# Moving the wait for the output DMAs behind the exit barrier in a two-part decode-attention kernel

## The chip, the cores and the metric

The kernel runs on one core of one Trainium2 chip. The metric is the device time of an execution in microseconds (us). A kernel is run several times. The profile shows one execution. Its *span* is the time from its first to its last instruction record, and it is shorter than the device time: what the runtime does before the first and after the last instruction has no records.

The engines are PE (TensorE), DVE (VectorE), ACT (ScalarE), POOL (GpSimd) and SP (SyncE, which issues nearly all DMAs here). A trailing q, as in POOLq, is an engine's sequencer.

## The reference

Two decode steps of attention for one token, one with a sliding window (A) and one over the whole cache (B), put side by side:

```python
# B = 1, Sq = 1, D = 576, 32 query heads, 16 key/value heads, cache of 8192 x 128, bfloat16
q = (x @ wq) as 32 heads of 128
scores = q . k * 128**-0.5          # A: the last 2048 positions, B: all 8192
o = softmax(scores) @ v
a_or_b = o as [1, 1, 4096] @ wo     # -> 576 values
return concatenate([a, b], axis=-1) # -> [1, 1, 1152]
```

## The kernel before

A small helper class records every operation with what it reads and writes, derives the semaphore waits, and then emits each engine's list inside one block. Only the end matters here.

```python
class Program:
    def emit(self):
        ...
        def plain(eng, ops):
            for op in ops:
                for key in sorted(op.left, key=str):
                    eng.wait_ge(self.sem(key), op.left[key][1])
                one(eng, op)
        ...
        with self.nc.Block() as block:      # its exit is a barrier of all five engines
            @block.sync
            def _(sp):
                run("sp", sp)
            @block.gpsimd
            def _(pool):
                run("pool", pool)
            ...                             # tensor, vector, scalar

...
    def finish_out(P):
        add("dve", lambda dve: dve.tensor_copy(outsb[:, P, :], ktps[P][:, 0:OUTW]), ...)
        ...
        add("sp", put, reads=[("outsb", P)], writes=[("out", P)], dma="out%d" % P)   # 1.1 KB to memory
...
    for P in range(2):
        for Q, lo, n, view, res, after in wo_loads:
            if Q == P:
                wo_part(P, lo, n, view, res)     # matmuls with the output weights, as they land
        finish_out(P)
    add("sp", lambda sp: sp.nop(), reads=[("out", 0), ("out", 1)])   # wait for both output DMAs
    prog.emit()
```

In the profile the block's exit has line L248: each engine drains, reports to GpSimd with a semaphore, and GpSimd releases all (its two EVENT_SEMAPHORE records).

Of the kernel before, what the change touches and what calls it, by code (L numbers as in the profile page):

```python
# [38 lines left out]
class Program:  # L39
# [15 lines left out]
    def add(self, eng, fn, reads=(), writes=(), dma=None, after=(), tag=None, inc=1, loop=None):  # L55
        op = Op(eng, fn, tuple(reads), tuple(writes), dma, tag, 16 if dma is not None else inc, loop)
        deps = []
        for r in op.reads:
            w = self.writer.get(r)
            if w is not None:  # L60
                deps.append((w, True))
            if r[0] == "bank":
                deps += [(o, False) for o in self.readers.get(r, ())]
        for r in after:
            deps += [(o, False) for o in self.readers.get(r, ())]
        for r in op.writes:
            w = self.writer.get(r)
            if w is not None:
                deps.append((w, False))
            deps += [(o, False) for o in self.readers.get(r, ())]  # L70
        for r in op.reads:
            self.readers.setdefault(r, []).append(op)
        for r in op.writes:
            self.writer[r] = op
            self.readers[r] = []
        for o, raw in deps:
            if o is op:
                continue
            if o.dma is None and o.eng == eng and (not raw or eng in ("pe", "sp")):
                continue  # L80
            op.deps.append(o)
            o.needed = True
        op.order = len(self.ops)
        self.ops.append(op)
        return op
# [184 lines left out]
def bass_concat_heads__sliding_block_cached__gqa_block_cached__decode_kernel(  # L270
# [27 lines left out]
    prog = Program(nc)  # L298
    add = prog.add
# [351 lines left out]
    def finish_out(P):  # L651
        add("dve", lambda dve: dve.tensor_copy(outsb[:, P, :], ktps[P][:, 0:OUTW]), reads=[("bank", P)],  # L652
            writes=[("outsb", P)])

        def put(eng):
            src = bass.AP(tensor=outsb, offset=P * OUTW, ap=[[32 * 2 * OUTW, 4], [1, OUTW]])
            dst = out[0, 0:1, P * DM:(P + 1) * DM].rearrange("o (j n) -> (o j) n", j=4)
            return eng.dma_start(dst, src)
        add("sp", put, reads=[("outsb", P)], writes=[("out", P)], dma="out%d" % P)


    for P in range(2):
# [11 lines left out]
        reads=["mask0", ("rows", 0)], writes=["maskS", "rows"])  # L674
# [47 lines left out]
    for P in range(2):  # L722
# [1 line left out]
            if Q == P:  # L724
                wo_part(P, lo, n, view, res)
        finish_out(P)
    add("sp", lambda sp: sp.nop(), reads=[("out", 0), ("out", 1)])
    prog.emit()

# [1 line left out]
_INS = ['A_x', 'A_k_cache', 'A_v_cache', 'A_wq', 'A_wo', 'B_x', 'B_k_cache', 'B_v_cache', 'B_wq', 'B_wo']  # L731
# [24 lines left out]
```

## Time and profile before

| | before |
|---|---|
| device time, median | 250.03 us (249.70 to 250.25, 5 runs) |
| span of the profiled execution | 247.66 us |
| memory traffic | 102.9 MB, 416 GB/s |
| end of the last matmul to the last record | 2.46 us (245.21 to 247.66) |

From the page of the kernel before, the span, the busy times and three rows of the table of 40 slices (tenths of busy time; GB/s moved):

```profile
span 247.7 us, 7505 instructions
...
PE 169.6 (68%) x3406; PEld 132.3 (53%) x3406; DVE 81.0 (33%) x152; ACT 87.1 (35%) x92; POOL 12.9 (5%) x49
...
PE   0193589994999559995999638998345144685634
...
DMA  7999999999999999999999999999999999999993
GB/s 270 406 433 431 430 431 421 426 423 429 431 425 429 426 421 431 422 431 434 423 429 429 423 431 429 426 437 426 429 429 423 431 426 429 434 427 427 421 406 138
```

The DMA engines are full in all slices but the first and last. The kernel is bound by memory traffic up to its last weights; only the first and the last few microseconds are anything else.

The end of it, from the timeline (start in us, duration in us, engine, line, operation):

```profile
245.26 0.31 DVE L652 CAST outsb<-ktps 128x144 bf16<-128x144 f32 x1 [10.17 <-PE ktps L646]
245.59 0.56 SPq L658 DMA_DIRECT2D out_dram<-outsb  x1
```

The wait for the outputs (L727) and the barrier at the block's exit (L248) by source line: engine, operation, count, shortest/median/longest duration in ns, and the starts of the first and the last in us:

```profile
L727 SPq EVENT_SEMAPHORE  x1: 17/17/17, 247.2 to 247.2; - x1
```

```profile
L248 POOLq EVENT_SEMAPHORE  x2: 17/17/17, 247.5 to 247.6; - x2
L248 POOLq DRAIN  x1: 322/322/322, 137.8 to 137.8; - x1
L248 ACTq DRAIN  x1: 326/326/326, 212.6 to 212.6; - x1
L248 PEldq DRAIN  x1: 370/370/370, 244.9 to 244.9; - x1
L248 DVEq DRAIN  x1: 347/347/347, 245.3 to 245.3; - x1
L248 SPq COMPARE_BRANCH  x1: 33/33/33, 247.3 to 247.3; - x1
L248 SPq DRAIN  x1: 13/13/13, 247.4 to 247.4; - x1
L248 SPq EVENT_SEMAPHORE  x1: 17/17/17, 247.6 to 247.6; - x1
L248 ACTq EVENT_SEMAPHORE  x1: 17/17/17, 247.6 to 247.6; - x1
L248 DVEq EVENT_SEMAPHORE  x1: 21/21/21, 247.6 to 247.6; - x1
L248 PEldq EVENT_SEMAPHORE  x1: 51/51/51, 247.6 to 247.6; - x1
```

And SyncE's waits (in us, count, longest):

```profile
SPq L727 <- DMA out_dram<-outsb: 1.0, 1, 1.0
...
SPq L248 <- PEq L248: 0.2, 1, 0.2
```

The order can be read off the starts. SyncE issues the last output DMA at 245.59 us. Its wait is met at 247.2 (247.217 in the instruction record, 1.63 us after the issue began). Only then does SyncE drain and report to the barrier, and GpSimd releases everyone at 247.6.

"Behind the issue" below means behind the start of the last output DMA. Figures with three decimals are from the instruction records of the traces, which the views round.

### The profile page before, as it was taken

The page shows a single profiled execution, that of the slowest core. Times are in us where ns is not written, and L with a number is a line of the kernel's source. Part 1 is how long each engine was busy: PE and PEld are TensorE (multiplying, and loading weights), DVE is VectorE, ACT ScalarE, POOL GpSimd, SP SyncE. Part 2 cuts the span into 40 slices and gives each one's busy share as a digit, 9 for nine tenths or more (in the row PEclk, how much of TensorE's full clock was granted, in tenths as well). Part 3 has the DMA queues.
Part 4 walks back from the last instruction along what each step waited for, and adds up shares of the span by engine and source line. Part 5 has one row for each costly group of instructions (what it writes and reads, how often), then busy time and mean ns, then how long its engine had stood idle before and what let it go on. Part 6 is the DMA issues. An engine that isn't in the chain of part 4 may idle for free. (4 is left out here: it accounts for less than half of the span.)

```text
span 247.7 us, 7505 instructions
## 1 busy us (share of the span) xinstructions
PE 169.6 (68%) x3406; PEld 132.3 (53%) x3406; DVE 81.0 (33%) x152; ACT 87.1 (35%) x92; POOL 12.9 (5%) x49
## 2 busy tenths in 40 slices
PE   0193589994999559995999638998345144685634
PEld 0031288763877458864878428785244142584522
DVE  0001225554555017564555122655004004204000
ACT  2000047767478009786578004775200000000000
POOL 7501000000000000000000000000000000000000
PEclk9999959999799979998899955999858755557555
DMA  7999999999999999999999999999999999999993
GB/s 270 406 433 431 430 431 421 426 423 429 431 425 429 426 421 431 422 431 434 423 429 429 423 431 429 426 437 426 429 429 423 431 426 429 434 427 427 421 406 138
DMA packets 8235, 102.92 MB, mean 416 GB/s; under 512 B 1184, under 2 KB 1312, under 8 KB 2080
## 3 DMA queue, kind: packets, MB, share of 16 engines
q1 hardware_dynamic: 7936, 102.77, 98.0%
q8 instruction: 8, 0.13, 0.2%
q10 hardware_dynamic: 288, 0.00, 0.1%
q14 instruction: 3, 0.02, 0.0%
HBM read 102.76 MB, written 0.00 MB: 415 GB/s over the span
## 5 line engine op out<-in xcount | busy, mean ns | idle before, releaser
L472 ACT ACTIVATE kt<-ktps 128x1024 bf16<-128x1024 bf16 x80 | 77.9, 1021 | 54.5 <-PE ktps L466 54.4
L466 PEld LDWEIGHTS ktps<-ident,kslots 128*128 128x128 bf16 x1280 | 78.9, 103 | 27.9 <-issue 27.9
L466 PE MATMUL ktps<-ident,kslots 128*128 128x128 bf16 x1280 | 85.1, 230 | 12.4 <-PEq L214 12.4
L475 DVE COPY kt<-ktps 128x1024 bf16<-128x1024 bf16 x80 | 55.2, 691 | 53.7 <-PE ktps L466 53.6
L557 PE MATMUL opsum<-vslots,ptm 128*32 128x128 bf16 x1280 | 28.1, 262 | 28.0 <-PEq L214 23.7
L557 PEld LDWEIGHTS opsum<-vslots,ptm 128*32 128x32 bf16 x1280 | 25.3, 119 | 31.6 <-issue 31.6
L486 PE MATMUL sacc<-kt,qst 128*32 128x512 bf16 x320 | 25.3, 392 | 1.8 <-PEq L214 1.8
L566 DVE TENSOR_TENSOR diag<-opsum,rows 128x512 f32<-128x512 f32 x5 | 3.5, 691 | 55.9 <-PE opsum L557 55.9
L425 PE MATMUL opsum<-vslots,xpad 128*32 128x512 bf16 x64 | 8.2, 489 | 14.8 <-DVE xpad L410 12.1
L599 ACT ACTIVATE stat<-stat 128x1 f32<-128x1 f32 (+1 forms) x2 | 0.6, 294 | 37.2 <-DVE stat L597 37.2
L425 PEld LDWEIGHTS opsum<-vslots,xpad 128*32 128x32 bf16 x64 | 2.3, 119 | 17.6 <-issue 13.1
L457 POOL COPY qst<-qtm 128x64 bf16<-128x64 bf16 x20 | 4.5, 236 | 123.2 <-PE sacc L486 113.5
L646 PE MATMUL ktps<-kslots,opj 128*32 128x144 bf16 x184 | 6.1, 326 | 5.8 <-DMA kslots<-in_B_wo_dram 3.9
L486 PEld LDWEIGHTS sacc<-kt,qst 128*32 128x32 bf16 x320 | 5.1, 94 | 8.2 <-issue 4.4
L431 ACT ACTIVATE qrow<-opsum 128x512 bf16<-128x512 f32 x2 | 1.2, 597 | 23.1 <-PE misc L425 23.1
L523 ACT ACTIVATE psb<-sacc,stat 128x2048 bf16<-128x2048 f32 x3 | 5.9, 1967 | 8.5 <-DVE stat L517 8.5
L646 PEld LDWEIGHTS ktps<-kslots,opj 128*32 128x32 bf16 x184 | 5.2, 145 | 6.4 <-DMA kslots<-in_B_wo_dram 4.2
L425 PE MATMUL misc<-vslots,xpad 128*32 128x512 bf16 x64 | 8.2, 487 | 0.0
L630 PE MATMUL misc<-acc,pick 128*128 128x32 f32 x16 | 3.8, 404 | 3.6 <-DVE acc L624 2.9
L433 DVE CAST qrow<-misc 128x512 bf16<-128x512 f32 x2 | 1.4, 692 | 14.6 <-PE misc L425 14.6
L652 DVE CAST outsb<-ktps 128x144 bf16<-128x144 f32 x2 | 0.6, 307 | 16.0 <-PE ktps L646 16.0
L630 PEld LDWEIGHTS misc<-acc,pick 128*128 128x128 f32 x16 | 3.6, 328 | 3.8 <-DVE acc L624 3.0
(66 smaller groups left out, 62.1 us busy)
## 6 DMA issues: line engine op xcount, KB each, us to landing
kslots<-in_B_k_cache_dram SPq DMA_DIRECT2D x16, 2048.0 KB, 19.6
vslots<-in_B_v_cache_dram SPq DMA_DIRECT2D x16, 2048.0 KB, 18.4
kslots<-in_A_k_cache_dram SPq DMA_DIRECT2D x4, 2048.0 KB, 29.8
vslots<-in_A_v_cache_dram SPq DMA_DIRECT2D x4, 2048.0 KB, 23.5
vslots<-in_A_wq_dram SPq DMA_DIRECT2D x2, 2048.0 KB, 9.9
vslots<-in_B_wq_dram SPq DMA_DIRECT2D x2, 2048.0 KB, 19.6
kslots<-in_A_wo_dram SPq DMA_DIRECT2D x2, 2016.0 KB, 23.8
kslots<-in_B_wo_dram SPq DMA_DIRECT2D x1, 2016.0 KB, 31.2
```

The lines of the kernel that those rows point to most:

```text
L425: ins = pe.matmul(qps[c][32 * j:32 * j + 32, :], lhsT=xpad[:, P, x, :], rhs=src[:, o:o + 512], start=(u == 0), stop=(u == WQ_UNITS - 1))
L433: add("dve", lambda dve: dve.tensor_copy(qrow[:, 512:1024], misc[:, :]), reads=[B_M], writes=[("qrow", 1)])
L457: add("pool", lambda pool: pool.tensor_copy(qst[:, s * 64:(s + 1) * 64], qtm[:, o:o + 64]), reads=[("qtm", KIND[g])], writes=[("qst", s)], ...
L466: ins = pe.matmul(ktps_bf[q][:, t * 128:(t + 1) * 128], lhsT=kslots[:, s, o:o + 128], rhs=ident[:, :], start=True, stop=True, is_transpose ...
L472: add("act", lambda act, q=q, dst=dst: act.activation(dst, ktps_bf[q], ACT.Copy), reads=[("bank", q)], writes=[("kt", u % NKT, q)], tag="e ...
L475: add("dve", lambda dve, q=q, dst=dst: dve.tensor_copy(dst, ktps_bf[q]), reads=[("bank", q)], writes=[("kt", u % NKT, q)], tag="e%d%d" % ( ...
L486: ins = pe.matmul(sacc[32 * j:32 * j + 32, 512 * half:512 * half + 512], lhsT=qst[:, s * 64 + e * 32:s * 64 + e * 32 + 32], rhs=rhs, start ...
L523: return act.activation(psb[:, :].rearrange("p (x g) -> p x g", g=2), src, ACT.Exp, bias=st(P, C_NB + k), scale=SCALE, accum_out=st(P, C_L ...
L557: ins = pe.matmul(opsum[32 * j:32 * j + 32, s * DH:(s + 1) * DH], lhsT=ptm[:, o:o + 32], rhs=vslots[:, s, b * 128:(b + 1) * 128], start=(u ...
L566: return dve.tensor_tensor(diag[:, g % 2, :, :], opsum[:, :].rearrange("p (s d) -> p d s", s=NS), m, ALU.mult)
L630: ins = pe.matmul(misc[:, 0:32], lhsT=pick[:, r, :], rhs=acc[:, d, 32 * r:32 * r + 32], start=(r == 0), stop=(r == 3))
L646: ins = pe.matmul(ktps[P][32 * j:32 * j + 32, 0:OUTW], lhsT=opj[:, P, jj:jj + 32], rhs=view[:, o:o + OUTW], start=(jj == 0), stop=(jj == H ...
```

## The change

The barrier shall not wait for the DMA's landing. SyncE reports to it right after the issue, and waits afterwards, as the program's last instruction.

```diff
         finish_out(P)
-    add("sp", lambda sp: sp.nop(), reads=[("out", 0), ("out", 1)])
     prog.emit()
+    for P in range(2):
+        o = prog.writer[("out", P)]
+        nc.sync.wait_ge(prog.sem(o.key), o.value)
```

## The prediction

> **What bounds the kernel now.** Memory traffic. In the page's slices the DMA engines are 90% busy or more in 38 of 40 slices at 406 to 437 GB/s, 102.9 MB in all; TensorE is busy 68%. The chain of waits that ended last closes with a 23.7 us DMA of weights, 0.7 us of matmuls, and a 0.31 us cast into `outsb` that begins at 245.26 us..
>
> **The tail, from the instructions of the lines concerned (us from the span's start).** SyncE issues the second output DMA from 245.59 to 246.15. Its packets are at the DMA engines from 246.79 to 246.86. SyncE's wait is met at 247.217; the view of SyncE's waits calls it 1.0 us; the first output landed long before. Then the exit of the block runs: branch 247.28, drain 247.44, GpSimd's semaphore instructions 247.48 and 247.56, every engine released at about 247.60, the last record (TensorE, 51 ns) ending at 247.664. So the exit costs 0.447 us behind the landing. The other four engines had drained by 245.7 at the latest; only SyncE's arrival is awaited.
>
> **What the change does.** It removes one NOP and moves the two waits behind the barrier. SyncE should reach its drain right after the issue: 246.15 plus 0.22 us (branch and drain as now) is 246.37, and the barrier is over at about 246.6. That lies 0.6 us before the landing. SyncE then waits until about 247.22 and the program ends there. The Trainium skill, "DMA: Bandwidth & Descriptors", section on the anatomy of one DMA, puts most of the fixed cost of a DMA into the write's receipt; this trace agrees in kind: 1.63 us from the start of the issue to the wait's end, 0.36 us of it after the last packet.
>
> **How much is critical.** All 0.447 us of the exit is on the critical path before; about 0.43 us should go, 0.17% of the time. The span should fall from 247.66 to about 247.23 us.
>
> From the span to the measured time 2.37 us are added (250.03 - 247.66), outside the records. The Trainium skill, "Runtime: NRT & Kernel Launch", section on the preamble and postamble breakdown, has a barrier of all engines and semaphore resets after the kernel; this trace doesn't show them. If they wait for all engines, SyncE decides and the gain is about 0.43 us. If not, the others, free 1.0 us earlier (247.6 to 246.6), could make it more. Three runs spread over 0.34 us. I predict 249.6 us, range 249.2 to 250.0; chance of faster by over 2% 0.005, within 2% 0.99, slower by over 2% 0.005.
>
> **What would show it.** Right: the view of SyncE's waits still has a wait for the landing of `out_dram`, shortened from 1.0 to about 0.6 us, now as the last record of the trace; the exit's semaphore instructions of all engines stand at about 246.6 us, before that landing; the landing stays about 1.63 us behind the issue's start.
>
> **What would make it wrong.** SyncE's drain may hold until its DMA has landed or its descriptors are processed (the drain now takes 13 ns, but with nothing in flight): then the barrier is not hidden and the gain is zero. Or the work behind the program may depend on something other than SyncE's end, and the gain of the span be lost or enlarged there. Or a shift of the DMA stream by some tenths of a us from run to run hides it all.

## More of the kernel before

ScalarE drained at 212.6 us, TensorE at 244.9 and VectorE at 245.3. GpSimd drained at 137.8 us and then waited more than 100 us, for SyncE in the end.

## The result, and the profile after

| | before | after |
|---|---|---|
| device time, median of 5 runs | 250.03 us | 249.14 us (249.03 to 249.18) |
| ratio of the fast runs | | 0.9966 (0.9954 to 0.9978) |
| span of the profiled execution | 247.66 us | 247.74 us |

The ratio is the mean time of one kernel's fast runs over that of the other's of the same rounds, so it is not quite the ratio of the medians. By it the change gains about 0.85 us, twice the predicted 0.43 us, and the median lies just outside the predicted range. The change is far below 2%, as predicted. The two profiled spans, oddly, hardly differ. From the page of the changed kernel:

```profile
span 247.7 us, 7504 instructions
...
GB/s 267 408 423 423 438 429 426 423 431 423 429 425 434 426 421 423 427 426 431 431 434 429 423 429 426 423 431 434 434 429 423 429 426 423 431 432 432 426 399 142
```

The timeline, the barrier and the last wait of the changed kernel:

```profile
245.75 0.31 DVE L652 CAST outsb<-ktps 128x144 bf16<-128x144 f32 x1 [10.44 <-PE ktps L646]
246.09 0.56 SPq L658 DMA_DIRECT2D out_dram<-outsb  x1
```

```profile
L248 POOLq EVENT_SEMAPHORE  x2: 17/17/17, 247.2 to 247.3; - x2
...
L248 PEldq DRAIN  x1: 372/372/372, 245.4 to 245.4; - x1
L248 DVEq DRAIN  x1: 347/347/347, 245.8 to 245.8; - x1
L248 SPq DRAIN  x1: 462/462/462, 246.7 to 246.7; - x1
L248 SPq EVENT_SEMAPHORE  x1: 17/17/17, 247.3 to 247.3; - x1
...
L248 PEldq EVENT_SEMAPHORE  x1: 51/51/51, 247.3 to 247.3; - x1
```

```profile
L730 SPq EVENT_SEMAPHORE  x1: 28/28/28, 247.7 to 247.7; - x1
```

```profile
SPq L730 <- DMA out_dram<-outsb: 0.4, 1, 0.4
SPq L248 <- PEq L248: 0.2, 1, 0.2
```

The DMA stream ended 0.5 us later in this execution (issue at 246.09 against 245.59), which hides the shorter tail in the span. Behind the issue, the span is shorter as predicted: the last record ended 2.073 us behind it before and 1.650 us now, 0.423 us less. The landing wait is met 1.62 us behind the issue (1.63 before). The barrier is now over before it: GpSimd releases the others at 247.3, and SyncE's wait, at 247.7, is the last record.

So the part inside the records is right, and about as much again was gained outside them. Each execution of a run has its time and its span (to 0.1 us) listed. Over nine runs of the kernel before, time minus span was 1.82 us on average; over five of the changed kernel on the same chip, 1.45 us. The two kernels differ only at their end, so something behind the program got 0.37 us shorter.

One detail of the inside was off: SyncE's drain took 462 ns directly behind the DMA's issue (13 ns before), so its landing wait shrank to 0.4 us, not to the predicted 0.6.

### The profile page after: what moved, and what is told of

It is laid out like the page before. It is cut to its first block, busy times and chain, and to the rows that moved or that the text cites. A ratio compares the mean times of both kernels' runs of the same rounds, so it can differ in the third digit from the quotient of the medians.

```text
span 247.7 us, 7504 instructions
## 1 busy us (share of the span) xinstructions
PE 169.6 (68%) x3406; PEld 131.4 (53%) x3406; DVE 80.9 (33%) x152; ACT 87.1 (35%) x92; POOL 12.9 (5%) x49
## 5 line engine op out<-in xcount | busy, mean ns | idle before, releaser
L557 PEld LDWEIGHTS opsum<-vslots,ptm 128*32 128x32 bf16 x1280 | 24.8, 118 | 32.1 <-issue 32.0
```

The costliest lines, as they stand in the source:

```text
L557: ins = pe.matmul(opsum[32 * j:32 * j + 32, s * DH:(s + 1) * DH], lhsT=ptm[:, o:o + 32], rhs=vslots[:, s, b * 128:(b + 1) * 128], start=(u ...
```

## The experiments

Four theories stood against each other.

- **A**: behind the program the runtime's ending (not recorded) has work on every engine, and another engine than SyncE needs longest. The early barrier frees that engine 0.78 us sooner (GpSimd's last record ends 1.986 us behind the issue before and 1.209 us after), and SyncE's later end doesn't count. Called A1 below if that engine is GpSimd, A2 if it is ScalarE or TensorE.
- **B**: SyncE's end decides. The gain is 0.43 us and the rest luck.
- **C**: it is the form of SyncE's last instructions that matters, not when the others leave.
- **D1/D2**, on the side: the 462 ns drain is a wait for the issued DMA (D1), or a fixed cost of a drain behind a DMA (D2).

The measure is the time of the profiled execution minus the start of its last output DMA, called T below. It leaves out the DMA stream's noise: two executions of the changed kernel in different runs gave 3.091 and 3.089 us. It is not always that exact: two executions in which GpSimd leaves at the same place gave 3.873 (before_again) and 3.916 us (both_waits). T and the remaining times below are counted from the span's start. If the device time begins before the first record, that piece is in all of them, so their absolute size is an upper limit. The edits are all at the program's end, so differences between runs are taken as free of it.

### after_again: the changed kernel again

No edit.

> The changed kernel once more, beside the kernel before on the same chip, to have spans of both. Theory A (behind the program the runtime's own ending is decided by engines other than SyncE, which the early barrier frees some 0.8 us sooner): the time is 0.75 to 1.0 us below the kernel before, and most of the loss beyond 0.43 us is in the part of the time behind the span (time minus span falls by 0.4 to 0.6 us). Theory B (SyncE's end decides; the rest of the 0.89 us was luck of the runs): 0.35 to 0.5 us below, time minus span unchanged.

The median was 248.87 us against 249.81 of before, ratio 0.9962 (0.9948 to 0.9975). Time minus span fell from 1.82 to 1.45 us, 0.37 us, a little less than the 0.4 to 0.6 us expected of A, but not the "unchanged" of B. The extra gain repeats.

### both_waits: waits on both sides of the barrier

```diff
     add("sp", lambda sp: sp.nop(), reads=[("out", 0), ("out", 1)])
     prog.emit()
+    for P in range(2):
+        o = prog.writer[("out", P)]
+        nc.sync.wait_ge(prog.sem(o.key), o.value)
```

> The waits stay in front of the barrier as in the kernel before and stand behind it a second time, where they are already met. Theory A (what counts is when the other engines leave the barrier): as the kernel before, 0 to 0.1 us above it. Theory C (it is the form of SyncE's last instructions, a wait as the last thing instead of a branch, a drain and a barrier, that shortens the ending): 0.4 us or more below the kernel before.

The median was 249.85 us against 249.81, ratio 0.9997 (0.9984 to 1.0011). SyncE again ends in a wait, and nothing is gained. C falls: the early barrier is needed.

### sp_late: SyncE held back in the kernel before

```diff
     prog.emit()
+    pad = nc.alloc_semaphore("pad_sp")
+    for _ in range(24):
+        nc.sync.sem_inc(pad, 1)
```

> The kernel before, with 24 semaphore increments on SyncE alone behind the barrier, 0.4 to 1.0 us of delay by an estimate from its 17 ns semaphore instructions; the trace gives the true delay D. Theory A (SyncE has slack of at least 0.37 us behind the barrier, the lag that it has in the changed kernel): the time rises by less than D, by D minus a slack of 0.37 us or more, so by at most D - 0.35. Theory B (SyncE's end decides): it rises by the whole D.

The increments of SyncE behind the barrier, by source line:

```profile
L731 SPq EVENT_SEMAPHORE  x24: 17/17/17, 248.1 to 249.9; - x24
```

They delay SyncE's last instruction by 1.90 us (3.931 us behind the issue, against 2.032 in before_again, below); one gap of 473 ns between two of them is part of that. The median rose by 1.40 us (251.21 against 249.81), and T by 1.38 us to 5.252 us. B wanted the full 1.90 us. SyncE has about 0.5 us of slack behind the barrier, and B falls. Held this late, SyncE decides, and the time ends 1.32 us behind its last instruction.

### others_late: the other four held back in the changed kernel

```diff
         nc.sync.wait_ge(prog.sem(o.key), o.value)
+    for k, (eng, n) in enumerate(((nc.gpsimd, 24), (nc.vector, 24), (nc.scalar, 24), (nc.tensor, 10))):
+        pad = nc.alloc_semaphore("pad%d" % k)
+        for _ in range(n):
+            eng.sem_inc(pad, 1)
```

> The changed kernel, with the other four engines held back behind the barrier by 24 semaphore increments each (TensorE 10), 0.4 to 1.0 us by estimate, SyncE untouched. Theory A: the gain shrinks by about the delay, so 0.4 us or more of the 0.89 us is lost. Theory B: with SyncE leaving 0.37 us behind the others, a delay D of the others costs D - 0.37 at the most; with D of 0.4 nothing is lost, with D of 0.8 some 0.4 us.

The median was 251.04 us, T 4.978 us. The increments lie 78 to 93 ns apart on GpSimd, ScalarE and VectorE (150 on TensorE), so the delay was about 1.9 us on GpSimd and 2.2 us on VectorE, more than estimated. With delays that large B allows nearly the same loss (2.22 minus SyncE's lag of 0.39 us) as A, and T rose by 1.89 us: this run does not tell A from B. (With the later runs known it fits A1: GpSimd's own delay was 1.88 us.) What it gave is the distance between the increments, and an upper limit for VectorE, which left last and was followed by only 1.49 us.

### pool_late, act_late, dve_late, pe_late: one engine held back in the kernel before

```diff
     prog.emit()
+    pad = nc.alloc_semaphore("pad")
+    for _ in range(13):               # act_late: 13 on nc.scalar, dve_late: 11 on nc.vector, pe_late: 7 on nc.tensor
+        nc.gpsimd.sem_inc(pad, 1)
```

> The kernel before with 13 semaphore increments on GpSimd alone behind the barrier, a delay D of about 1.0 us (an estimate from the 78 ns from one to the next that the run others_late shows). Measured as the time minus the start of the last output DMA in the profiled run, which was 3.92 us in both_waits and 3.09 us in the changed kernel. Theory A1 (GpSimd decides the ending): rises by D to about 4.9 us. Theory A2 (ScalarE or TensorE decides): rises by D minus GpSimd's slack, so by less than D. Theory B (SyncE): no rise until D is over its slack, which B cannot name.

> The same with 13 increments on ScalarE alone (78 ns each by others_late, D about 1.0 us). A2 with ScalarE deciding: the time minus the start of the last output DMA rises by D from 3.92 us to about 4.9 us; with GpSimd or TensorE deciding: by less than D.

> The same with 11 increments on VectorE alone (93 ns each by others_late, D about 1.0 us). In others_late VectorE left last and the time ended 1.49 us behind it, against 1.83 us in the changed kernel, so VectorE has at least 0.34 us of slack: a rise of at most 0.7 us, to 4.6 us or less.

> The same with 7 increments on TensorE alone (150 ns each by others_late, D about 1.05 us). If TensorE decides: a rise by D, from 3.92 us to about 4.95 us; if GpSimd or ScalarE decides: less. In the changed kernel the time ends 1.79 us behind TensorE's last instruction, so its own remaining work is 1.79 us at most.

GpSimd's increments in pool_late, by source line:

```profile
L731 POOLq EVENT_SEMAPHORE  x13: 17/17/17, 247.7 to 248.6; - x13
```

The same line in act_late, dve_late and pe_late, one of each:

```profile
L731 ACTq EVENT_SEMAPHORE  x13: 17/17/17, 247.8 to 248.8; - x13
...
L731 DVEq EVENT_SEMAPHORE  x11: 21/21/21, 248.0 to 248.9; - x11
...
L731 PEldq EVENT_SEMAPHORE  x7: 51/51/51, 249.1 to 250.0; - x7
```

The table counts from T = 3.873 us of before_again (next section); D is by how much the held engine's last record moved; "remaining" is the time from that record to the end of the device time.

| engine held | run | D | T | rise of T | slack (D - rise) | remaining |
|---|---|---|---|---|---|---|
| GpSimd | pool_late | 1.012 | 4.974 | 1.101 | none | 1.972 |
| TensorE | pe_late | 1.051 | 4.760 | 0.887 | 0.16 | 1.631 |
| ScalarE | act_late | 1.009 | 4.560 | 0.687 | 0.32 | 1.515 |
| VectorE | dve_late | 1.015 | 4.532 | 0.659 | 0.36 | 1.470 |
| SyncE | sp_late | 1.899 | 5.252 | 1.379 | 0.52 | 1.321 |

The medians were 250.67, 250.79, 250.69 and 250.57 us in the order of the table's first four rows, against 249.91 of before; they are too noisy to rank the engines. By T only GpSimd's delay comes through whole: A1. The other four have slack, SyncE the most.

The table takes one execution per run, and GpSimd's rise is 0.09 us above its delay there. All executions of these runs settle that: in each the held engine leaves last, so time minus span is its remaining time. On average it is 1.93 us for GpSimd (2.02, 1.88, 1.90, 1.92; the first is the profiled one), 1.67 for TensorE, 1.56 for ScalarE, 1.50 for VectorE and 1.35 for SyncE. The kernel before has 1.81 us over its 33 fast executions beside the experiments, which puts its T at about 3.89 us. Counted so, GpSimd's rise is about 1.04 us for a delay of 1.01, so most of the 0.09 us was the one execution; the other four keep slacks of about 0.14, 0.29, 0.34 and 0.51 us. In the other profiled executions where GpSimd decides, 1.88 to 1.93 us remain behind it.

### before_again: the kernel before, with its time and trace from one execution

No edit.

> The kernel before itself, so that the time and the trace of one and the same execution are known. From the runs so far: the time ends 1.88 to 1.97 us behind GpSimd's last instruction (three runs where it was among the last) and that stands 1.986 us behind the start of the last output DMA, so the time minus the start of that DMA should be 3.87 to 3.96 us. If it is 3.5 us or less (the value that the 0.42 us of the shortened span would need), theory A falls.

The last output DMA in the timeline, and GpSimd's release by source line:

```profile
245.54 0.56 SPq L658 DMA_DIRECT2D out_dram<-outsb  x1
```

```profile
L248 POOLq EVENT_SEMAPHORE  x2: 17/17/17, 247.4 to 247.5; - x2
```

T was 3.873 us, at the low end of A's range. The time was 249.41 us and the span 247.615 us, 1.795 us apart. (The median, 249.80 against 249.88 of before in the same rounds, ratio 0.9998, 0.9985 to 1.0012, shows no bias of the comparison.) The change therefore takes 3.873 - 3.090 = 0.783 us off the tail, and GpSimd's last record moves by 1.990 - 1.209 = 0.781 us.

### pool_alone_late: GpSimd alone put back in the changed kernel

```diff
         nc.sync.wait_ge(prog.sem(o.key), o.value)
+    pad = nc.alloc_semaphore("pad")
+    for _ in range(10):
+        nc.gpsimd.sem_inc(pad, 1)
```

> The changed kernel with 10 semaphore increments on GpSimd alone behind the barrier (78 ns each in others_late, 0.78 us), which puts GpSimd's last instruction back to where the kernel before has it, 1.99 us behind the start of the last output DMA (1.21 us in the changed kernel), while the other three and SyncE leave as early as in the changed kernel. If the gain is the early release of GpSimd and of nothing else: time minus DMA start goes from 3.09 back to 3.87 to 3.96 us and the whole gain is gone. If TensorE or any other engine shares in it: 3.4 to 3.7 us. If SyncE decides: it stays 3.09 us.

The start of the last output DMA in the timeline, and GpSimd's ten increments by source line:

```profile
246.27 0.56 SPq L658 DMA_DIRECT2D out_dram<-outsb  x1
```

```profile
L733 POOLq EVENT_SEMAPHORE  x10: 17/17/17, 247.5 to 248.2; - x10
```

GpSimd's last record ends 1.992 us behind the issue, as in the kernel before (1.990). All others leave as early as in the changed kernel. T was 3.876 us, and before_again had 3.873. The median was 250.03 us against 250.12, ratio 0.9994 (0.998 to 1.0008); one run of the kernel before took 375 us and is left out. The whole gain is gone with GpSimd's release alone.

### sp_held_before_drain: what the drain behind the DMA waits for

```diff
         finish_out(P)
+    pad = nc.alloc_semaphore("pad")
+    def hold(sp):
+        for _ in range(8):
+            ins = sp.sem_inc(pad, 1)
+        return ins
+    add("sp", hold)
     prog.emit()
```

> The changed kernel with 8 semaphore increments of SyncE (58 ns each in the run sp_late, 0.46 us) between the issue of the last output DMA and the drain at the block's end. Theory D1 (the drain's 0.462 us is a wait for the issued DMA, over at a fixed time about 1.08 us behind the issue's start): the drain shrinks to some ten ns, the barrier and the time keep their places, time minus DMA start 3.09 us. Theory D2 (a drain behind a DMA costs 0.46 us wherever it stands): all moves by 0.46 us, to 3.5 us.

The barrier's line in this run:

```profile
L248 POOLq EVENT_SEMAPHORE  x2: 17/17/17, 247.3 to 247.4; - x2
...
L248 SPq DRAIN  x1: 13/13/13, 247.3 to 247.3; - x1
```

The drain fell from 462 to 13 ns, and GpSimd's last record moved by only 0.046 us (1.209 to 1.255 us behind the issue); T was 3.157 us (3.09 without the hold). D1 holds: directly behind the issue the drain waits for something that is over about 1.08 us behind the issue's start, shortly before the DMA's first packets (1.19 us behind it in the changed kernel). It is a wait, not a fixed cost; what it waits for is not shown, but it is not the landing, which came at 1.63 us.

### early_barrier: the last piece of work behind the barrier too

```diff
-        per = {e: [o for o in self.ops if o.eng == e] for e in self.ENGINES}
+        per = {e: [o for o in self.ops[:self.cut] if o.eng == e] for e in self.ENGINES}
+        late = {e: [o for o in self.ops[self.cut:] if o.eng == e] for e in self.ENGINES}
 ...                                     # behind the block:
+        for name, eng in (("pe", self.nc.tensor), ("dve", self.nc.vector), ("sp", self.nc.sync)):
+            plain(eng, late[name])
 ...
     for P in range(2):
+        if P == 1:
+            prog.cut = len(prog.ops)
```

> The changed kernel, with the whole last piece (the matmuls with the second weights, the cast, the output DMA and the waits) emitted behind the block's exit barrier, which then falls into the wait for those weights, at about 235 us. Theory A with the remaining work of each engine as measured (GpSimd 1.9 us, TensorE 1.63, ScalarE 1.52, VectorE 1.47, SyncE 1.32 behind its last instruction): GpSimd is free long before, SyncE decides now, at 1.65 + 1.32 = 2.97 us behind the start of the last output DMA, 0.12 us less than the changed kernel's 3.09, so a time about 1.0 us below the kernel before. Theory B (SyncE decided already): 3.09 us, no gain over the changed kernel.

The barrier (L249 in this file) and the last output DMA:

```profile
L249 POOLq EVENT_SEMAPHORE  x2: 17/17/17, 236.7 to 236.7; - x2
...
L249 SPq DRAIN  x1: 429/429/429, 236.2 to 236.2; - x1
...
L249 ACTq EVENT_SEMAPHORE  x1: 17/17/17, 236.8 to 236.8; - x1
...
L249 PEldq EVENT_SEMAPHORE  x1: 51/51/51, 236.8 to 236.8; - x1
```

```profile
246.00 0.56 SPq L663 DMA_DIRECT2D out_dram<-outsb  x1
```

The barrier is over at 236.8 us, more than 9 us before the last output DMA is issued. GpSimd no longer counts. T was 2.985 us (2.97 expected), and 1.324 us of it lie behind SyncE's last record, the 1.32 us of sp_late. So SyncE decides now, and 0.105 us more is off the tail than in the changed kernel. In the device time that is too little to see: the median was 248.98 us against 249.88 of before, ratio 0.9962 (0.9948 to 0.9975), the same ratio as after_again had on another chip. Time minus span, over all five executions of each, agrees with the shorter tail (1.32 against 1.45 us in after_again, with SyncE's last record at the same place behind the issue). It is the best tail, but it is not shown to be the faster kernel.

## Why the prediction was wrong

- **The bound, the order of the tail, the size of the exit: right.** The exit cost 0.447 us behind the landing, the DMA's landing stayed 1.62 us behind the issue, and the span behind the issue fell by 0.423 us (0.43 predicted).
- **"SyncE should reach its drain right after the issue: 246.15 plus 0.22 us (branch and drain as now)": wrong in size.** The drain took 462 ns instead of 13. The prediction named this as a risk. The barrier ended 1.3 us behind the issue instead of 1.0, still before the landing, so it cost nothing in the span. But it held GpSimd as well, and so it cost part of the gain, at most some 0.1 us: early_barrier, where GpSimd leaves long before the end, has a T of 2.985 instead of 3.090 us.
- **"If they wait for all engines, SyncE decides and the gain is about 0.43 us": the step that failed.** The outside of the records was taken as a constant that follows the program's last instruction. It is not one. In these runs each engine has its own remaining time, and the latest end, counted from each engine's own last instruction, decides. GpSimd needs 1.88 us or more and SyncE 1.32. Before, all left together at 2.0 us behind the issue and GpSimd decided, at 1.99 + 1.88 = 3.87. After, GpSimd ended at 1.21 + 1.88 = 3.09 and SyncE would only need 1.65 + 1.32 = 2.97. The gain is GpSimd's 0.78 us, not SyncE's. The prediction's next sentence had the right branch ("If not, the others, free 1.0 us earlier (247.6 to 246.6), could make it more"), but its number was not built on it.
- **"2.37 us are added": wrong.** It set the median of the times against the span of one execution whose own time is not on record. In one execution the two are 1.80 us apart (before_again), and 1.75 to 1.92 us in the 33 others listed.
- **The Trainium skill, "Runtime: NRT & Kernel Launch", section "The ~15µs preamble/postamble breakdown"**, has a closing barrier that waits for all engines (about 1.5 us) and semaphore resets on every engine. A barrier fed by five engines with different distances fits what the delays show, but no record of these traces lies behind the last instruction. That GpSimd's late part is there is shown by the time; what it does there is not, and stays open.
- The ratio puts the gain at 0.85 us, the tail at 0.78 us. The difference is within the interval of the ratio.

## What to carry to other kernels

The exit barrier holds engines that have long been idle, and an engine that leaves late can put off the end of the whole execution: here GpSimd, drained since 137.8 us, was held to the end, and 1.88 us or more followed its last instruction. So put into the barrier only what the other engines really wait for, and let the landing of the last output be waited for by one engine behind it. Here that engine, SyncE, was also the one with the least left to do. When a change alters *when engines leave*, don't take the time outside the records as a constant: compare time and span of the same execution, and delay one engine at a time to find the one that decides. Measure such a tail from a fixed event near the end, because the stream in front of it is noisier (some 0.7 us from run to run here) than the effect.

## What the Trainium skill lacked or had wrong

- "Runtime: NRT & Kernel Launch", "The ~15µs preamble/postamble breakdown": it gives the ending as one sequence of about 1.5, 1.5 and 2 us. Here time minus span was only 1.32 to 1.97 us in all in the profiled executions, and the time left differs by which engine decides: 1.88 to 1.97 us behind GpSimd's last instruction, 1.63 behind TensorE's, 1.52 behind ScalarE's, 1.47 behind VectorE's, 1.32 behind SyncE's. The page has no split by engine. (The metric here may stop before the resets end; no run shows it.)
- "VectorE: DVE Perf Modes", "The DRAIN you can't avoid": it tells two things called DRAIN apart, VectorE's pipeline flush and the runtime's boilerplate of about 12 ns on all engines. The drains of the program's own block exit are neither, and are lacking there: SyncE's took 13 ns with nothing in flight, but 462 ns directly behind a DMA issue; the other engines' took 322 to 372 ns in the kernels before and after.
- "DMA: Bandwidth & Descriptors": no section says that a drain of the issuing engine waits, until about 1.08 us behind the start of the issue in the changed kernel (1.15 in early_barrier, where the issue took 0.65 instead of 0.56 us), but not for the landing (1.62 us). Its fixed cost of about 2.0 us is a fit for another kind of queue (GpSimd's); the 1.1 KB output DMA here took 1.62 us from the start of the issue to the met wait, 1.19 us of it before its first packet and 0.35 us behind its last.
- No page has the pace of a chain of semaphore increments: mostly one every 58 ns on SyncE, 78 on GpSimd and ScalarE, 93 on VectorE, 150 on TensorE (sp_late, others_late); single gaps were longer, 473 ns once on SyncE and 247 ns once on TensorE.
